# Attention and a gated feed-forward block on one core: batches 0 and 1 are transposed by TensorE and their reciprocals spread by a selector matmul

## The chip, the cores and the metric

The kernel runs on one core of a Trainium2 chip. The core has a matrix engine (TensorE, PE in the profile, with its weight loads as PEld), a vector engine (DVE), a scalar engine (ACT), a general engine (POOL) that here mainly issues loads, and a queue processor (SP) that issues the other transfers. The metric is the time of one execution on the device in microseconds.

## The reference

```python
B, H, S, D = q.shape                      # 8, 8, 576, 64
scores = scale * np.matmul(q, k.transpose(0, 1, 3, 2))
mask = (rel >= 0) & (rel < window)        # window 128
scores = np.where(mask, scores + bias[None], -1000000000.0)   # bias: -slope[h] * |rel|
attn = np.exp(scores - max)
attn = attn / (np.sum(attn, axis=-1, keepdims=True) + 1e-09)
x = (attn @ v), heads side by side        # 4608 tokens x 512
g = x @ w_gate                            # 512 x 1536
gelu = 0.5 * g * (1.0 + erf(g * inv_sqrt2))
val = x @ w_val                           # 512 x 1536
return (gelu * val @ w_out)               # 1536 x 512
```

Inputs and output are fp32.

## The kernel before

A batch (576 tokens) has five key blocks j of 128 keys; block 0 is half filled. Heads go in pairs, c = 0 to 3, with i the head in the pair. q, k and v of a batch are loaded by POOL with a cast to bf16 (L80, five loads each). Staging tiles `qs` and `ks` have one buffer; their transposes `qT`, `kT` have two. Batch 0 is transposed by TensorE (L101) and copied by DVE (L104), all others by a DMA transpose that SP issues (L110).

`scores0`, `scores1` and `scores2` compute the scores transposed, keys on partitions (L119). ACT takes the exp into `P` (L126), and DVE multiplies by the decay-and-window mask (L129), which comes in two layouts, `emask` and `emask2`. `sums` multiplies `P` by a block of ones, 48 matmuls of 32 columns each (L180), so that row 32c+16i and the 15 after it hold the sums of one head. DVE takes reciprocals (L187, L188) into `r`. To have each head's row on 64 partitions, SP writes eight rows of `r` to memory (`rd`, L192) and reads them back spread (`rb`, L194). `values` multiplies `P` by v (L205), and DVE scales the result with `rb` into `xT` (L211), the feed-forward's input, features on partitions.

The feed-forward goes in nine groups g of 512 tokens. `gate_val` makes one of twelve 128-feature steps f: four matmuls with `wg`, four with `wv` (L224), a gelu on ACT (L228), a product on DVE (L229). `out_half` is six matmuls with `wo` (L239); after two of them ACT copies the bank (L244) and SP stores it (L246). A group needs the attention of batches up to g (for g of 1 or more). Between the gates and the end of a group the program puts steps of the attention of later batches among the eight out halves.

The program sets the order on each engine; nothing reorders it. Every engine and SP's queue work through their instructions in turn. All matmul results go through eight PSUM banks handed out in turn by `bank()`, so a matmul can wait for the reader of a result eight banks earlier. POOL's loads have eight completion semaphores in turn, so a load waits for the one eight before. `P` has three buffers, each for two pairs.

The lines around which the start turns, before the loop over the groups (L303 to L315):

```python
load_qk(1)
load_v(0)
...
transposes_dma(1)
sums(0)
for n in range(4):
    todo.pop(0)[1]()
for c in range(4):
    values(0, c)
```

Of the kernel before, what the change touches and what calls it, by code (L numbers as in the profile page):

```python
# [19 lines left out]
PCOL = (512, 0, 256, 704, 960)  # L20

QS = 320
# [3 lines left out]
def kernel(  # L26
# [23 lines left out]
    p_pool = ctx.enter_context(tc.tile_pool(name="pp", bufs=3))  # L50
# [17 lines left out]
    ones = consts.tile([128, 2, 32], BF16, name="ones")  # L68
# [62 lines left out]
    def scores0(b, c):  # L131

        P = p_pool.tile([128, 2, 2, 1088], BF16, name="P")
        probs[b, c] = P
        ps = [bank(), bank()]
        for m in (0, 1):
            for i in (0, 1):
                score(b, c + m, i, 4, ps[i], 128 * m)
        for i in (0, 1):
            exp(P[:, :, i, 960:1088], ps[i][:, 0:256].rearrange("p (m n) -> p m n", m=2))  # L140

    def scores1(b, c):
        P = probs[b, c - c % 2][:, c % 2]
        ps = [bank(), bank()]
# [3 lines left out]
        for i in (0, 1):  # L148
            exp(P[:, i, 0:512], ps[i])
        mask(P[:, :, 0:512].rearrange("p i (n x) -> p i n x", n=2),  # L150
             emask[:, 2 * c:2 * c + 2, :].unsqueeze(2).to_broadcast((128, 2, 2, 256)))

    def scores2(b, c):
        P = probs[b, c - c % 2][:, c % 2]
        ps = [bank(), bank()]
        for j in (0, 3):
            for i in (0, 1):
                score(b, c, i, j, ps[i], 256 * (j // 3))
        for i in (0, 1):
# [13 lines left out]
    def sums(b):  # L173

        ps = [bank(), bank()]
        for j in range(5):
            for s, a, e, col in pieces(j):
                for i in (0, 1):
                    for c in range(4):
                        nc.tensor.matmul(  # L180
                            out=ps[s][32 * c:32 * c + 32, a - QS * s:e - QS * s],
                            lhsT=ones[:, i, :],
                            rhs=probs[b, c - c % 2][:, c % 2, i, col:col + e - a],
# [5 lines left out]
        rb = r_pool.tile([128, 4, S], FP32, name="rb")  # L189
        recip[b] = rb  # L190
        d = d_pool.tile([4, 2, S], FP32, name="rd")
        nc.sync.dma_start(out=d.rearrange("c i s -> (c i) s"), in_=r[0:128:16, :])  # L192
        for i in (0, 1):
            nc.sync.dma_start(  # L194
                out=rb[64 * i:64 * i + 64, :, :],
                in_=d[:, i, :].unsqueeze(0).to_broadcast((64, 4, S)))

    def values(b, c):
        P = probs[b, c - c % 2][:, c % 2]
        ps = [bank(), bank()]  # L200
# [49 lines left out]
    for t in (qs, ks):  # L250
# [3 lines left out]
        base=0, pattern=[[-1, 128]], channel_multiplier=1)  # L254
    load_qk(0)
    relt = consts.tile([128, 256], mybir.dt.int32, name="relt")
    tmpl = consts.tile([128, 256], FP32, name="tmpl")
    nc.gpsimd.iota(relt, pattern=[[1, 256]], base=0, channel_multiplier=-1)
    nc.gpsimd.tensor_copy(out=tmpl, in_=relt)
    for base, step, chan in ((0, 1, -1), (W - 1, -1, 1)):  # L260
        nc.gpsimd.affine_select(
            out=tmpl, in_=tmpl, compare_op=ALU.is_ge, fill=1e9,
            base=base, pattern=[[step, 256]], channel_multiplier=chan)
# [3 lines left out]
    nc.vector.memset(ones, 0.0)
    for i in range(2):
        nc.vector.memset(ones[:, i, 16 * i:16 * i + 16], 1.0)
    nc.vector.memset(emask2[0:64, :, 0:192], 0.0)  # L270

    def masks(c):
        for h in (2 * c, 2 * c + 1):
            slope = 2.0 ** (-8.0 * (h + 1) / H)
            nc.scalar.activation(out=emask[:, h, :], in_=tmpl, func=AF.Exp, scale=-slope)
        e, e2 = emask[:, 2 * c:2 * c + 2, :], emask2[:, 2 * c:2 * c + 2, :]
        nc.vector.tensor_copy(out=e2[64:128, :, 0:192], in_=e[64:128, :, 64:256])
        nc.vector.tensor_copy(out=e2[:, :, 192:448], in_=e)
# [105 lines left out]
```

## Time and profile before

| | us |
|---|---|
| median of 3 runs | 430.2 (428.4 to 431.09) |
| profiled execution, its own time | 431.19 |
| its span, first to last instruction | 429.4 |
| PE busy | 352.6 (82%) |
| DVE busy | 183.6 (43%) |
| ACT busy | 176.0 (41%) |
| POOL busy | 109.6 (26%) |
| mean granted clock of TensorE | 0.927 |

Busy shares are means over the whole span. They say little about a stretch in which all engines wait for one transfer; those are found in the page's slices and then in the timeline, in which each row gives a start, a duration, an instruction, and in brackets how long its engine stood before it and what ended that.

### The profile page before, as it was taken

Reading aid. Unit: us, or ns where it says so; the run is one execution under the profiler, and the core shown is the slowest. Engines: PE = TensorE matmul, PEld = TensorE weight load, DVE = VectorE, ACT = ScalarE, POOL = GpSimd, SP = SyncE. Lnnn points to the kernel's source line nnn. Section 1 sums busy time; section 2 is a strip of 40 time slices with the busy share of each in tenths; the row PEclk is TensorE's granted clock in tenths of the full one; section 3 lists DMA queues with packets and bytes.
Section 4 is the critical chain, followed back from the end, with each engine's and each line's share of the span. In section 5 each row is a group of like instructions: output and inputs, shape, how many; then the busy total and the mean of one; then the engine's idle time right before and its main releaser. Section 6 shows DMA issues by size and latency. Waiting matters only on the chain. (4 is left out here: it accounts for less than half of the span.)

```text
span 429.4 us, 6083 instructions
## 1 busy us (share of the span) xinstructions
PE 352.6 (82%) x2385; PEld 164.5 (38%) x2424; DVE 183.6 (43%) x281; ACT 176.0 (41%) x326; POOL 109.6 (26%) x138
## 2 busy tenths in 40 slices
PE   1640033997789697999999999999999999999996
PEld 0320031443334344444444344444444444444442
DVE  2580013245444466554645464545556450430330
ACT  1540031236533672428534842665285322322321
POOL 9394230917126103029005500920000000000000
PEclk9955556799989998999999999999999999999999
DMA  9499999999699939589679929994801502002002
GB/s 87 31 134 120 180 199 229 143 173 129 124 170 129 58 52 183 105 169 150 85 175 133 159 62 231 100 141 104 156 27 51 136 0 82 17 0 99 1 2 98
DMA packets 164269, 47.48 MB, mean 111 GB/s; under 512 B 149840, under 2 KB 155472, under 8 KB 164240
## 3 DMA queue, kind: packets, MB, share of 16 engines
q0 software_dynamic: 118288, 18.88, 59.3%
q1 hardware_dynamic: 45952, 28.20, 28.7%
q8 instruction: 19, 0.31, 0.3%
q14 instruction: 10, 0.08, 0.1%
HBM read 47.19 MB, written 9.58 MB: 132 GB/s over the span
## 5 line engine op out<-in xcount | busy, mean ns | idle before, releaser
L229 DVE TENSOR_TENSOR hT<-ps,gelu 128x512 bf16<-128x512 f32 x108 | 74.7, 691 | 126.4 <-PE ps L224 126.3
L224 PE MATMUL ps<-xT,wg 128*128 128x512 bf16 x431 | 114.1, 386 | 7.7 <-DMA wo<-in_moe_w_out_dram 6.9
L228 ACT ACTIVATE gelu<-ps 128x512 bf16<-128x512 f32 x108 | 64.5, 597 | 129.3 <-PE ps L224 129.0
L224 PE MATMUL ps<-xT,wv 128*128 128x512 bf16 x415 | 110.4, 384 | 0.7 <-issue 0.2
L239 PE MATMUL ps<-wo,hT 128*128 128x512 bf16 x411 | 99.8, 382 | 2.6 <-issue 1.9
L126 ACT ACTIVATE P<-ps 128x512 bf16<-128x512 f32 (+2 forms) x160 | 72.9, 555 | 46.8 <-PE ps L119 46.6
L129 DVE TENSOR_TENSOR P<-P,emask 128x1024 bf16<-128x1024 bf16 x64 | 46.0, 724 | 67.1 <-ACT P L126 67.1
L224 PEld LDWEIGHTS <-wg 128*128 128x128 bf16 x432 | 41.4, 99 | 58.9 <-issue 10.7
L224 PEld LDWEIGHTS <-wv 128*128 128x128 bf16 x432 | 42.8, 99 | 53.3 <-issue 3.1
L80 POOL DMA_DIRECT2D qs<-in_q_dram x40 | 33.7, 859 | 113.7 <-DMA qT<-qs 93.5
L239 PEld LDWEIGHTS <-hT 128*128 128x128 bf16 x432 | 38.7, 98 | 49.6 <-issue 9.4
L119 PE MATMUL ps<-qT,kT 64*128 64x256 bf16 (+1 forms) x320 | 27.4, 284 | 33.8 <-DMA qT<-qs 30.2
L244 ACT COPY osb<-ps 128x512 f32<-128x512 f32 x36 | 21.2, 588 | 63.2 <-PE ps L239 41.6
L80 POOL DMA_DIRECT2D vb<-in_v_dram x40 | 33.8, 894 | 47.5 <-PE ps L205 38.4
L211 DVE TENSOR_TENSOR xT<-ps,rb 128x320 bf16<-128x320 f32 x64 | 25.4, 449 | 21.7 <-DMA rb<-rd 20.9
L80 POOL DMA_DIRECT2D ks<-in_k_dram x40 | 33.8, 897 | 0.0
L119 PEld LDWEIGHTS <-kT 64*128 64x128 bf16 x320 | 11.7, 101 | 53.2 <-issue 47.8
L205 PE MATMUL ps<-P,vb 128*64 128x128 bf16 (+2 forms) x384 | 21.7, 259 | 3.7 <-DVE xT L211 3.7
L180 PE MATMUL ps<-P,ones 128*32 128x128 bf16 (+2 forms) x384 | 13.7, 270 | 13.4 <-DVE P L129 13.1
L205 PEld LDWEIGHTS <-vb 128*64 128x64 bf16 x384 | 16.0, 117 | 14.1 <-issue 13.8
L187 DVE RECIPROCAL r<-ps 128x320 f32<-128x320 f32 x8 | 17.3, 2157 | 5.7 <-PE ps L180 5.7
L180 PEld LDWEIGHTS <-ones 128*32 128x32 bf16 x384 | 10.2, 107 | 18.1 <-issue 17.9
(32 smaller groups left out, 65.7 us busy)
## 6 DMA issues: line engine op xcount, KB each, us to landing
rb<-rd SPq DMA_DIRECT2D x16, 576.0 KB, 7.9
out_dram<-osb SPq DMA_DIRECT2D x36, 256.0 KB, 5.0
qs<-in_q_dram POOLq DMA_DIRECT2D x32, 128.0 KB, 4.3
ks<-in_k_dram POOLq DMA_DIRECT2D x32, 128.0 KB, 4.4
vb<-in_v_dram POOLq DMA_DIRECT2D x32, 128.0 KB, 5.2
wg<-in_moe_w_gate_dram POOLq DMA_DIRECT2D x4, 384.0 KB, 21.0
wv<-in_moe_w_val_dram POOLq DMA_DIRECT2D x4, 384.0 KB, 23.0
wo<-in_moe_w_out_dram POOLq DMA_DIRECT2D x1, 1536.0 KB, 28.6
```

Source lines behind the costliest of these rows:

```text
L80: nc.gpsimd.dma_start(out=t[lo:128, j, :].rearrange("p (h d) -> p h d", h=H), in_=src[b][:, 128 * j - 64 + lo:128 * j + 64, :].rearrange(" ...
L119: nc.tensor.matmul(out=ps[:, col:col + 128 * n].rearrange("p (n t) -> p n t", n=n), lhsT=kT[b % 2][lo:lo + 64, j, c, :], rhs=qT[b % 2][lo: ...
L126: nc.scalar.activation(out=dst, in_=src, func=AF.Exp, scale=0.125)
L129: nc.vector.tensor_tensor(out=dst, in0=dst, in1=m, op=ALU.mult)
L180: nc.tensor.matmul(out=ps[s][32 * c:32 * c + 32, a - QS * s:e - QS * s], lhsT=ones[:, i, :], rhs=probs[b, c - c % 2][:, c % 2, i, col:col ...
L205: nc.tensor.matmul(out=ps[s][64 * i:64 * i + 64, a - QS * s:e - QS * s], lhsT=vb[b % 2][:, j, 64 * h:64 * h + 64], rhs=P[:, i, col:col + e ...
L211: nc.vector.tensor_tensor(out=xT[:, c, b * S + lo:b * S + hi], in0=ps[s][:, 0:hi - lo], in1=recip[b][:, c, lo:hi], op=ALU.mult)
L224: nc.tensor.matmul(out=ps, lhsT=w[:, c, 128 * f:128 * (f + 1)], rhs=xT[:, c, t0:t0 + 512], start=(c == 0), stop=(c == 3))
L228: nc.scalar.activation(out=gl, in_=pg, func=AF.Gelu)
L229: nc.vector.tensor_tensor(out=hid[g][:, f, :], in0=pv, in1=gl, op=ALU.mult)
L239: nc.tensor.matmul(out=po, lhsT=hid[g][:, f, 128 * t:128 * (t + 1)], rhs=wo[:, f, :], start=(f == 0), stop=(f == NF - 1))
L244: nc.scalar.copy(out=osb, in_=po)
```

## The change

Batches 0 and 1 are transposed by TensorE, and the copies of the transposes are shared between ACT and DVE. `qs` and `ks` get second buffers. Two ways now lead from `r` to `rb`: `spread_dma`, as before, for batches 2 to 7, and `spread_pe` for batches 0 and 1, eight fp32 matmuls with a constant 0/1 matrix `sel`, each copied out of its bank by ACT. The scores of a pair are made in one visit that takes four banks, and the scores of key block 4 of all four pairs in one visit of two. The mask has one layout: the block of ones for key block 0 holds zeros for the missing keys instead. `P` is per pair with six buffers. The order in the groups is written out as lists. From group 3 on, the sums of a batch stand after the first gate step and its values after the ninth and eleventh.

```diff
-    p_pool = ctx.enter_context(tc.tile_pool(name="pp", bufs=3))
+    p_pool = ctx.enter_context(tc.tile_pool(name="pp", bufs=6))
+    p4_pool = ctx.enter_context(tc.tile_pool(name="p4", bufs=2))
...
-    emask2 = consts.tile([128, H, 576], BF16, name="emask2")
+    sel = consts.tile([128, 4, 2, 64], FP32, name="sel")
-    qs, ks = (consts.tile([128, 5, DM], BF16, name=f"{nm}s") for nm in "qk")
+    qs, ks = ([consts.tile([128, 5, DM], BF16, name=f"{nm}s{i}") for i in range(2)]
+              for nm in "qk")
...
+    def scores0(b):
+        P = p4_pool.tile([128, 4, 2, 128], BF16, name="P4")
+        ps = [bank(), bank()]
+        for c in range(4):
+            for i in (0, 1):
+                score(b, c, i, 4, ps[i], 128 * c)
+        for i in (0, 1):
+            exp(P[:, :, i, :], ps[i].rearrange("p (c n) -> p c n", c=4))
+        mask(P.rearrange("p c i n -> p (c i) n"), emask[:, :, 0:128])
+    def scores(b, c):
+        ps = [bank() for _ in range(4)]
...
+        for n in (0, 1):
+            for i in (0, 1):
+                exp(P[:, i, 512 * n:512 * n + 512], ps[2 * n + i])
+            mask(P[:, :, 512 * n:512 * n + 512].rearrange("p i (n x) -> p i n x", n=2), e)
...
+    def spread_pe(b, r):
+        for lo, hi in ((0, QS), (QS, S)):
+            for c in range(4):
+                ps = bank()
+                nc.tensor.matmul(
+                    out=ps[:, 0:hi - lo], lhsT=sel[:, c, :, :].rearrange("p i m -> p (i m)"),
+                    rhs=r[:, lo:hi], start=True, stop=True)
+                nc.scalar.copy(out=recip[b][:, c, lo:hi], in_=ps[:, 0:hi - lo])
...
     load_qk(0)
+    load_qk(1)
+    load_v(0)
...
+    copies = (nc.scalar.copy, nc.vector.tensor_copy)
+    for c in (0, 1):
+        transposes(0, c, copies)
+    scores(0, 0)
+    for c in (2, 3):
+        transposes(0, c, (nc.vector.tensor_copy, nc.vector.tensor_copy))
+    scores0(0)
+    for c in (1, 2, 3):
+        scores(0, c)
...
-    transposes_dma(1)
-    sums(0)
-    for n in range(4):
-        todo.pop(0)[1]()
-    for c in range(4):
-        values(0, c)
+    r = sums(0)
+    for c in (0, 1):
+        transposes(1, c, (nc.scalar.copy, nc.scalar.copy))
+    spread_pe(0, r)
+    for c in range(4):
+        scale(0, c, values(0, c))
+    for c in (2, 3):
+        transposes(1, c, copies)
...
+            if 3 <= g < B - 1:
+                if f == 0:
+                    run(("sum", g + 1))
+                elif f in (8, 10):
+                    run(("pv", g + 1, f - 8, f - 7))
+        if g == 0:
+            todo = [("s0", 1), ("s", 1, 0), 0, 1, ("s", 1, 1), 2, 3, ("s", 1, 2), 4, ("s", 1, 3),
+                    5, 6, ("sum", 1), ("pv", 1, 0, 1, 2, 3), 7]
+        elif g == 1:
+            todo = [("s0", 2), ("s", 2, 0), 0, ("s", 2, 1), 1, ("s", 2, 2), 2, ("s", 2, 3), 3,
+                    ("s0", 3), 4, ("sum", 2), ("s", 3, 0), 5, 6, ("s", 3, 1), 7,
+                    ("pv", 2, 0, 1, 2, 3)]
+        elif g == 2:
+            todo = [("s", 3, 2), 0, ("s", 3, 3), 1, 2, ("s0", 4), ("sum", 3), ("s", 4, 0), 3, 4,
+                    ("s", 4, 1), 5, ("pv", 3, 0, 1), ("s", 4, 2), 6, ("pv", 3, 2, 3),
+                    ("s", 4, 3), 7]
+        elif b < B:
+            todo = [("s0", b), ("s", b, 0), 0, 1, ("s", b, 1), 2, 3, ("s", b, 2), 4, 5,
+                    ("s", b, 3), 6, 7]
```

Three places show what the lists move. The first is the start of SP's queue, before:

```order
L110 DMA_TRANSPOSE kT_93<-ks 128x20x128
L110 DMA_TRANSPOSE qT_91<-qs 128x20x128
L192 DMA rd<-r 8x576
L194 DMA rb<-rd 64x4x576 x2
L110 DMA_TRANSPOSE kT_92<-ks 128x20x128
L110 DMA_TRANSPOSE qT_90<-qs 128x20x128
L246 DMA out_dram<-osb 128x512
```

and now:

```order
L112 DMA_TRANSPOSE kT_97<-ks_93 128x20x128
L112 DMA_TRANSPOSE qT_95<-qs_91 128x20x128
L261 DMA out_dram<-osb 128x512 x4
L112 DMA_TRANSPOSE kT_98<-ks_94 128x20x128
L112 DMA_TRANSPOSE qT_96<-qs_92 128x20x128
L261 DMA out_dram<-osb 128x512 x2
L196 DMA rd<-r 8x576
```

Before, the queue began with the transposes of batch 1 and the reciprocals of batch 0. Now its first rows are the transposes of batch 2, and the first `rd` is that of batch 2.

The second is the same queue in the steady groups, one group before:

```order
L246 DMA out_dram<-osb 128x512
L110 DMA_TRANSPOSE kT_93<-ks 128x20x128
L110 DMA_TRANSPOSE qT_91<-qs 128x20x128
L246 DMA out_dram<-osb 128x512 x3
L192 DMA rd<-r 8x576
L194 DMA rb<-rd 64x4x576 x2
```

and now:

```order
L261 DMA out_dram<-osb 128x512 x3
L112 DMA_TRANSPOSE kT_98<-ks_94 128x20x128
L112 DMA_TRANSPOSE qT_96<-qs_92 128x20x128
L196 DMA rd<-r 8x576
L198 DMA rb<-rd 64x4x576 x2
L261 DMA out_dram<-osb 128x512 x4
```

`rd` and `rb` stood ahead of a group's last store and of the next group's transposes. They now stand behind both transposes.

The third is DVE after the gates of group 1, before (`emask_87` is the second mask layout):

```order
L129 TENSOR_TENSOR P<-P,emask 128x2x512
L129 TENSOR_TENSOR P<-P,emask_87 128x2x576
L187 RECIPROCAL r<-ps 128x320
L188 RECIPROCAL r<-ps 128x256
L129 TENSOR_TENSOR P<-P,emask 128x2x512
L129 TENSOR_TENSOR P<-P,emask_87 128x2x576
L129 TENSOR_TENSOR P<-P,emask 128x2x512
L129 TENSOR_TENSOR P<-P,emask_87 128x2x576
L211 TENSOR_TENSOR xT<-ps,rb 128x320
```

and now:

```order
L131 TENSOR_TENSOR P_1164<-P_1164,emask 128x1024
L131 TENSOR_TENSOR P<-P,emask 128x2x512 x8
L131 TENSOR_TENSOR P_1286<-P_1286,emask 128x1024
L189 RECIPROCAL r<-ps 128x320
L190 RECIPROCAL r<-ps 128x256
L131 TENSOR_TENSOR P<-P,emask 128x2x512 x4
L226 TENSOR_TENSOR xT<-ps,rb 128x320
```

Nine or ten masks now come before the reciprocals of batch 2, where four came before, and four masks still lie between the reciprocals and the first scaling.

## Rows read from the trace of the kernel before

**Rows 1.** Page, 40 equal slices: busy tenths of PE.
```profile
PE   1640033997789697999999999999999999999996
```

**Rows 2.** Timeline 0:75: start, duration, engine, line, instruction, count, [idle before <-releaser].
```profile
28.12 1.97 PE L180 MATMUL ps<-P,ones 128*32 128x192 bf16 x45 [2.13 <-DVE P L129]
...
35.98 14.72 SPq L110 DMA_TRANSPOSE qT<-qs  x1
...
60.33 2.10 PE L119 MATMUL ps<-qT,kT 64*128 64x128 bf16 x20 [30.24 <-DMA qT<-qs]
...
72.23 3.01 DVE L211 TENSOR_TENSOR xT<-ps,rb 128x320 bf16<-128x320 f32 x8 [6.33 <-DMA rb<-rd]
73.10 2.04 PE L224 MATMUL ps<-xT,wg 128*128 128x512 bf16 x3 [6.90 <-DMA wo<-in_moe_w_out_dram]
```

**Rows 3.** Timeline of POOL: template selects, loads and waits of the start.
```profile
10.81 0.86 POOL L261 TENSOR_SCALAR_AFFINE_SELECT tmpl<-tmpl 128x256 f32<-128x256 f32 x2
18.71 4.23 POOL L80 DMA_DIRECT2D qs<-in_q_dram  x5 [7.03 <-PE ps L101]
...
31.25 0.81 POOL L93 DMA_DIRECT2D wg<-in_moe_w_gate_dram  x1
...
49.15 0.69 POOL L80 DMA_DIRECT2D vb<-in_v_dram  x1 [1.27 <-DMA wv<-in_moe_w_val_dram]
...
64.09 0.88 POOL L80 DMA_DIRECT2D qs<-in_q_dram  x1 [1.22 <-DMA wv<-in_moe_w_val_dram]
```

**Rows 4.** Timeline 0:75: the first transposes and exps.
```profile
13.38 0.29 PE L101 MATMUL ps<-ident,ks 128*128 128x128 bf16 x1 [0.55 <-DMA ks<-in_k_dram]
...
13.46 0.74 PE L101 MATMUL ps<-ident,qs 128*128 128x128 bf16 x5
...
19.27 1.95 ACT L126 ACTIVATE P<-ps 128x512 bf16<-128x512 f32 x4
```

**Rows 5.** Lines by form: line, engine, operation, shapes, count | busy us, mean ns | idle.
```profile
L129 DVE TENSOR_TENSOR P<-P,emask 128x1024 bf16<-128x1024 bf16 x32 | 22.1, 691 | 51.7 <-ACT P L126 51.7
...
L244 ACT COPY osb<-ps 128x512 f32<-128x512 f32 x36 | 21.2, 588 | 63.2 <-PE ps L239 41.6 <-issue 21.7
...
L187 DVE RECIPROCAL r<-ps 128x320 f32<-128x320 f32 x8 | 17.3, 2157 | 5.7 <-PE ps L180 5.7
L188 DVE RECIPROCAL r<-ps 128x256 f32<-128x256 f32 x8 | 13.6, 1695 | 0.0
...
L126 ACT ACT_TABLE_LOAD x6 | 7.7, 1283 | 0.1
...
L104 DVE COPY qT<-ps 128x640 bf16<-128x640 bf16 x4 | 1.9, 486 | 6.9 <-PE ps L101 6.9
```

**Rows 6.** Windows: PE, PEld, DVE, ACT, POOL busy, PE clock, DMA share, GB/s.
```profile
120.00:125.00 5.00, 4.84 (x18) 1.98 (x17) 2.13 (x7) 2.47 (x3) 2.62 (x3) 0.66 1.18 82
```

**Rows 7.** Timelines 60:130 to 185:230: loop starts, and rd to scaled xT.
```profile
121.61 1.92 PE L224 MATMUL ps<-xT,wg 128*128 128x512 bf16 x4
...
154.65 0.62 SPq L192 DMA_DIRECT2D rd<-r  x1
...
164.84 1.55 DVE L211 TENSOR_TENSOR xT<-ps,rb 128x320 bf16<-128x320 f32 x4 [5.98 <-DMA rb<-rd]
...
172.82 1.03 PE L224 MATMUL ps<-xT,wg 128*128 128x512 bf16 x4
...
211.91 1.03 PE L224 MATMUL ps<-xT,wg 128*128 128x512 bf16 x4
```

**Rows 8.** Timeline 185:230: a transpose on SP's queue, a pair's values.
```profile
218.07 6.77 SPq L110 DMA_TRANSPOSE kT<-ks  x1
...
222.36 0.66 PE L205 MATMUL ps<-P,vb 128*64 128x192 bf16 x12
```

**Rows 9.** Timeline of PE from 340: the out matmuls of group 7, the first gates of group 8.
```profile
383.79 10.52 PE L239 MATMUL ps<-wo,hT 128*128 128x512 bf16 x47
394.15 1.03 PE L224 MATMUL ps<-xT,wg 128*128 128x512 bf16 x4
```

More of the change, by code (lines that the diff above doesn't have):

```diff
@@ L18 @@
 Q0 = (0, 64, 192, 320, 448)
[L20 removed]
+PCOL = (576, 0, 256, 768)
 QS = 320
@@ L95, in load_w, with transposes @@
                 in_=src[:, lo:hi].rearrange("(c p) f -> p c f", p=128))
-    def transposes(b, c):
-        for src, dst in ((qs, qT), (ks, kT)):
+    def transposes(b, c, copies):
+        for src, dst, copy in ((ks, kT, copies[0]), (qs, qT, copies[1])):
             ps = bank().bitcast(BF16)
@@ L176, in sums @@
         for j in range(5):
-            for s, a, e, col in pieces(j):
+            for s, a, e, lo in pieces(j):
                 for i in (0, 1):
@@ L254 @@
         base=0, pattern=[[-1, 128]], channel_multiplier=1)
-    load_qk(0)
[L256 to L263, printed above, removed]
+    tmpl = consts.tile([128, 256], FP32, name="tmpl")
@@ new lines @@
+    nc.gpsimd.iota(tmpl, pattern=[[1, 256]], base=0, channel_multiplier=-1,
+                   allow_small_or_imprecise_dtypes=True)
+    for half, base, step, chan in ((0, 0, 1, -1), (1, -1, -1, 1)):
+        t = tmpl[:, 128 * half:128 * half + 128]
+        nc.gpsimd.affine_select(
+            out=t, in_=t, compare_op=ALU.is_ge, fill=1e9,
+            base=base, pattern=[[step, 128]], channel_multiplier=chan)
+    load_qk(0)
+    load_qk(1)
+    load_v(0)
+    nc.vector.memset(ones, 0.0)
+    for i in range(2):
+        nc.vector.memset(ones[64:128, 0, i, 16 * i:16 * i + 16], 1.0)
+        nc.vector.memset(ones[:, 1, i, 16 * i:16 * i + 16], 1.0)
@@ L264 @@
+    nc.vector.memset(sel, 0.0)
     for i in range(2):
         nc.vector.memset(vb[i][0:64, 0, :], 0.0)
[L267 to L278, printed above, removed]
-        nc.vector.tensor_copy(out=e2[:, :, 448:576], in_=e[:, :, 0:128])
@@ L307, with run @@
         load_w(step * n, step * (n + 1))
-    nc.gpsimd.dma_start(out=wo, in_=moe_w_out.rearrange("(c p) f -> p c f", p=128))
-    load_v(1)
-    transposes_dma(1)
-    sums(0)
-    for n in range(4):
-        todo.pop(0)[1]()
-    for c in range(4):
-        values(0, c)
-    def fetch(b):
+    r = sums(0)
[6 more added lines that the diff above has]
+        transposes(1, c, copies)
+    for n in range(2):
+        nc.gpsimd.dma_start(
+            out=wo[:, 6 * n:6 * n + 6, :],
+            in_=moe_w_out[768 * n:768 * n + 768, :].rearrange("(c p) f -> p c f", p=128))
+    load_v(1)
+    def run(item):
+        what, b, *c = item
+        if what == "s0":
+            scores0(b)
+        elif what == "s":
+            scores(b, c[0])
+        elif what == "sum":
+            r = sums(b)
+            if b == 1:
+                spread_pe(b, r)
+            else:
+                spread_dma(b, r)
+        elif what == "pv":
+            for x in c:
+                scale(b, x, values(b, x))
+    for g in range(NG):
+        b = g + 2
         if b < B:
```

132 lines of the change are left out of this document (44 added, 88 removed).

## The prediction, made before the change was run

> **What bounds the kernel now.** I began with the slices of the page [rows 1]: TensorE (PE) is busy nine tenths or more from the seventeenth slice on, and nearly all of its idle time lies before that, in slices 1 to 7 and in a few dents up to 172 us. So the time is a start-up, three uneven groups of tokens, and a saturated rest. The timeline says what the start-up waits for [rows 2]: the sums of batch 0 end at 30.1, then PE stands for 30.2 us until the DMA transpose of qT lands. That transpose was issued at 35.98 and shares the DMA engines with the weights: these are issued from 31.25 on, and POOL's waits show wv's first quarter landed at 49.2 and its last at 64.1 [rows 3]. The reciprocals go through memory behind it, so xT comes at 72.2 and the first gate matmul starts at 73.1. From there I read the loop starts: gates of group 1 at 121.6, of group 2 at 172.8, of group 3 at 211.9 [rows 7]. The 39.1 us of the last interval repeats up to group 5. A pure group costs 48 out matmuls in 394.15 - 383.79 = 10.4 us [rows 9], 0.216 each, so 96 gate matmuls cost 20.7 and a group 31.1.
>
> **The new start, step by step.** Call T0 the first gate matmul (73.1 now).
> 1. iota and two selects now run ahead of the q loads. Two selects of twice the width took 0.86 [rows 3], so with the iota about 1.0 us. The last k tile was transposed at 13.4 [rows 4]; now 14.4. Fifteen transposes follow; five took 0.74 with their tail [rows 4], so about 2.0: done at 16.4.
> 2. First exps at 16.9. Four exps take 1.95 [rows 4]: 18.9, mask 0.69 [rows 5]: 19.6. Then DVE copies four transposes at 0.49 [rows 5]: 21.5. Only then can the scores of key block 4 run (all four pairs), so ACT stands about 3 us, and works 14 exps at 0.49 = 6.9 from 22.0 to 28.9; last mask 29.6. The twelve copies that built the second mask are gone from DVE, but ACT is the slower here, and they gain nothing.
> 3. Sums: 1.97 at low clock [rows 2], the first reciprocal starts 1.2 into them: 30.8 + 2.16 + 1.70 [rows 5] = 34.7. Meanwhile PE makes 20 transposes of batch 1, about 3 us, to 34.6: they hide the reciprocals.
> 4. The spread: eight fp32 matmuls, each copied out by ACT. No row shows an fp32 matmul. Lower end: one pass like bf16, 0.216 x 320/512 and x 256/512, 1.0 us for eight. Upper end: a column as dear as in the slowest fp32 row, the reciprocals, 4 x (2.16 + 1.70) = 15.4. I take 4.0, half a microsecond each, near the copy of 512 fp32 columns at 0.59 [rows 5], because each product must leave by such a copy: 38.6. The Trainium skill (FP8 and Floating Point Precision, TensorE Precision Notes) says that true FP32 takes four passes through the array. By it the eight cost an estimated 3.9 us at the full clock and 7.8 at half; the sum would then be the same or 3.8 higher.
> 5. Values of four pairs, 0.66 each at full clock [rows 8], somewhat more here: 3.1, to 41.7. DVE scales a pair in 0.78 (four pieces in 1.55 [rows 7]), hidden but for the last. Twenty transposes of batch 1 stand ahead of the gates: 2.3. **T0 = 44.0**, 29.1 earlier.
>
> Do the loads keep up? POOL stood 7.0 us before q of batch 1, for the one buffer of q and k [rows 3]; with a second one it doesn't, so the weights are issued from 24.5, not 31.25. Six quarters took 64.1 - 49.2 = 14.9, 2.5 each, so from about 31 to 49; a pair of quarters feeds three gate steps, 5.2 us. No wait if that pace holds.
>
> **The groups after it** (t from the last gate matmul; sums at full clock 1.1; scores of a batch 9,216 columns, two heads side by side, 2.1).
> - Group 0: PE work is scores 2.1, out 10.4, sums 1.1, spread 4.0, values 2.6 = 20.2. ACT needs 1.3 for its table [rows 5], 0.5 for the last gelu, 8.8 for 18 exps and about 1 for two copies, so the last mask comes 1.1 after PE wants it; then PE stands 1.8 for the first reciprocal, as nothing lies between sums and spread. 23.1 + 20.7 = 43.8, against 48.5 now, which held a slow start (its first three gate matmuls took 2.04 [rows 2]) and two waits.
> - Group 1: sums of batch 2 start at 12.2 (ACT again); the reciprocals wait for a mask, end at 17.4. From rd's issue to the first scaled xT took 164.84 - 154.65 = 10.2 [rows 7]: 27.6. PE has then long made the rest and all four values (20.8): it stands 7.6. Scaling follows pair by pair, the first gate ends about 1.6 late, and after such a stop the clock is low: behind the stop that ended group 0 it was 0.66 from 120 to 125 [rows 6], worth 1.7. 31.5 + 20.7 = 52.2, against 51.2.
> - Group 2: sums of batch 3 start at 6.5 and rb is used at 22.2. PE gets to the third score of batch 4 by 14.3, where the banks held by two unscaled values stop it for 8.3. Then 4.4 of work, 27.0, and 1.5 for the clock. 49.2, **against 39.1**: the change gives back 10 here, because a batch and a half of scores stand in it and the way of the reciprocals through memory is no longer covered by gates.
> - Groups 3 to 5: 31.1 + sums 1.1 + values 2.6 + scores 2.1 + 0.6 = 37.5, against 39.1; the difference is the wait of the sums for the last mask. Here rd stands on SP behind both transposes: the first took 6.8 on the queue [rows 8] with rb in flight ahead, the second less, so rd goes at 8 to 10.5 into the loop, and scaled xT comes at 18 to 20.7. PE would stop for it only from about 20.5, when the third pair's values want banks. I take no stop.
> - Groups 6, 7, 8: 34.8 + 31.1 + 31.1 = 97.0, last copy and store 4.0 (429.4 less the end of the last out matmul, 394.2 + 31.1), against 34.0 (what is left of the span) + 62.2 + 4.0.
>
> Differences: start -29.1, group 0 -4.7, group 1 +1.0, group 2 +10.1, groups 3 to 5 -4.8, group 6 +0.8: **-26.7**. Against the profiled execution, 431.2 us with a span of 429.4, that is 404.5; the median of the runs is 1.0 lower, so **404 us**.
>
> **Rivals.**
> - A. The fp32 products stream several times while the clock is low. For: the 48 sums took 1.97 there [rows 2], near twice what the columns cost at 0.216 per 512. Against: sums and transposes keep PE busy for 5 us before. Doubling the 4.0 taken above: T0 +4, 408. Chance 0.15. The rule on four passes quoted from the Trainium skill in step 4 would make it so.
> - B. The loads set the start after all: then the wait for the transpose only hid one for the weights. For: in this trace wv's first quarter landed at 49.2 [rows 3]. Against: it was issued 7 us later than it will be, beside two DMA transposes that are gone. T0 = 49.2 and some microseconds for wo, which would come last: 409 to 414. Chance 0.12.
> - C. rb comes later than 20.5 into groups 3 to 6 by 1 to 3 us: four times that, 408 to 416. Chance 0.10.
> - D. **Slower than before**: the same place on SP, but rd and rb fall behind transposes as slow as qT's first, which took 24 us from issue to use [rows 2]. The point is the 20.5 us above; each microsecond beyond it costs four in sum, and +31 is reached when scaled xT comes 28 into the loop. 435. Against: that one shared the engines with all the weights, a later one took 6.8 on the queue [rows 8]. Chance 0.02.
> - E. Better than summed: PE slips past the stop in group 2, or starts at 40: 393 to 399. Chance 0.13.
> Left for the forecast, 399 to 408: 0.45; 0.03 for the upper end of the fp32 cost, +11 at each spread (427).
>
> A change under 1% cannot be told from none here. Faster by over 1%: all but D and a part of the last and of what I overlook, 0.94; same 0.03; slower 0.03. The range 393 to 416 takes in E, A, B and most of C.
>
> **What will show it.** The 30 us hole of PE after the sums gone, and gates from about 44 (48 says A, 49 with waits on wg or wv says B). Eight fp32 matmuls near 0.5 us each. DVE waiting on rb before xT at the end of groups 1 and 2, with PE idle about 8 us in each, and a low clock behind it. Loops of 37.5 in groups 3 to 5, with DVE but not PE waiting for rb (PE waiting says C). The forecast fails if the stops of groups 1 and 2 are missing, or if T0 lies outside 40 to 49.

## The result, and the profile after the change

| | before | after |
|---|---|---|
| median, us | 430.1 (4 runs, 428.4 to 431.1) | 408.7 (4 runs, 406.6 to 409.6) |
| profiled execution, its own time | 431.19 | 409.64 |
| its span | 429.4 | 407.8 |
| PE busy | 352.6 (82%) | 359.6 (88%) |
| mean granted clock of TensorE | 0.927 | 0.944 |

The ratio of after to before is 0.9499, 95% interval 0.9452 to 0.9547: 21.4 us faster. The forecast was 404, its range 393 to 416. The time lies inside the range, and the sum still holds one large error.

The table gives the start of the first gate matmul and then the length of each group's loop, gate start to gate start, in us. All rows but the predicted one are read from timelines of PE.

| | first gate | g0 | g1 | g2 | g3 | g4 | g5 | g6 | g7 |
|---|---|---|---|---|---|---|---|---|---|
| before | 73.1 | 48.5 | 51.2 | 39.1 | 39.1 | 39.1 | 39.1 | 33.9 | 31.1 |
| predicted | 44.0 | 43.8 | 52.2 | 49.2 | 37.5 | 37.5 | 37.5 | 34.8 | 31.1 |
| after | 41.0 | 43.2 | 49.0 | 51.4 | **47.6** | 37.4 | 37.4 | 34.6 | 31.1 |

So the start gave 32.1 us and groups 2 and 3 gave 12.3 and 8.5 of that back. Groups 0, 1, 4 and 5 are shorter by 5.3, 2.2, 1.7 and 1.7, and group 6 is longer by 0.7. Group 3 should have been one of three equal loops and is 10.2 longer than its neighbours.

First the slices of the page of after, which answer to [rows 1]. Each digit is the busy share of a fortieth of the span in tenths; PEclk is the granted clock.

```profile
PE   0569999899992899949929999999999999999996
...
PEclk9958999999997699979977999999999999999999
...
DMA  9999999999918990199959984967110502002002
```

The hole of slices 4 to 7 is gone. Three dents are left, in slices 13, 18 and 21 (about 130, 180 and 210 us), each with a low clock beside it. The last one is new: nothing stood there before.

The start, from the timeline of all engines (start, duration, engine, line, instruction, count, idle before and its releaser); it answers to [rows 2]:

```profile
29.14 1.97 PE L183 MATMUL ps<-P,ones 128*32 128x192 bf16 x45 [1.64 <-DVE P L131]
...
30.30 2.16 DVE L189 RECIPROCAL r<-ps 128x320 f32<-128x320 f32 x1 [1.21 <-PE ps L183]
...
33.16 4.77 PE L206 MATMUL ps<-r,sel 128*128 128x320 f32 x16
...
37.86 2.06 PE L217 MATMUL ps<-P,vb 128*64 128x192 bf16 x48
...
40.98 1.03 PE L239 MATMUL ps<-xT,wg 128*128 128x512 bf16 x4
```

PE doesn't stop between the sums and the gates. The spread takes 4.77 us; the profile counts two instructions for each product, so x16 are the eight of the code. It starts at 33.16, behind the first twenty transposes of batch 1, which hide the reciprocals: those of the first 320 columns are there at 32.46, and the first four products need no others.

POOL's timeline at the same time, which answers to [rows 3]:

```profile
23.79 0.95 POOL L96 DMA_DIRECT2D wg<-in_moe_w_gate_dram  x1
...
30.23 0.83 POOL L319 DMA_DIRECT2D wo<-in_moe_w_out_dram  x1 [0.30 <-DMA wg<-in_moe_w_gate_dram]
32.17 0.82 POOL L319 DMA_DIRECT2D wo<-in_moe_w_out_dram  x1 [1.11 <-DMA wv<-in_moe_w_val_dram]
```

The weights are issued 7.5 us earlier. Their first quarters have landed by 30.2 and 32.2, where wv's landed at 49.2 before. The gates don't wait for them.

PE's timelines around the dents:

```profile
133.21 2.77 PE L239 MATMUL ps<-xT,wg 128*128 128x512 bf16 x4 [8.59 <-DVE xT L226]
...
140.62 1.03 PE L239 MATMUL ps<-xT,wg 128*128 128x512 bf16 x4
...
179.69 0.64 PE L217 MATMUL ps<-P,vb 128*64 128x128 bf16 x6 [5.12 <-DVE xT L226]
...
213.78 2.02 PE L217 MATMUL ps<-P,vb 128*64 128x192 bf16 x24 [7.65 <-DVE xT L226]
215.74 1.89 PE L239 MATMUL ps<-xT,wg 128*128 128x512 bf16 x4
```

The first stop ends group 1 (8.59), the second lies in group 2 (5.12), the third in group 3 (7.65). All three wait for a scaled xT. The 16 gate matmuls behind the first one took 140.62 - 133.21 = 7.4 us, where 16 at 0.216 are 3.5. Around the third stop the clock was low too, by the windows (PE, PEld, DVE, ACT, POOL busy, then the granted clock):

```profile
212.00:217.00 5.00, 3.22 (x28) 2.12 (x28) 3.77 (x9) 0.00 (x0) 1.65 (x3) 0.50 0.07 6
```

DVE's timeline says what the scaling before the third stop waited for:

```profile
213.23 1.55 DVE L226 TENSOR_TENSOR xT<-ps,rb 128x320 bf16<-128x320 f32 x4 [10.92 <-DMA rb<-rd]
```

So what is late stands on SP's queue. Its timeline in group 3 (from 184.6) and in group 4 (from 232.2), which answers to [rows 8]:

```profile
186.06 5.87 SPq L112 DMA_TRANSPOSE kT<-ks  x1
192.09 7.40 SPq L112 DMA_TRANSPOSE qT<-qs  x1
199.55 1.24 SPq L196 DMA_DIRECT2D rd<-r  x1
205.45 1.25 SPq L198 DMA_DIRECT2D rb<-rd  x2
...
233.58 3.21 SPq L112 DMA_TRANSPOSE kT<-ks  x1
236.92 3.51 SPq L112 DMA_TRANSPOSE qT<-qs  x1
240.96 0.63 SPq L196 DMA_DIRECT2D rd<-r  x1
243.12 1.26 SPq L198 DMA_DIRECT2D rb<-rd  x2
```

The same chain runs at about half the speed in group 3. The two transposes take 13.3 us instead of 6.7, and from rd to rb it is 5.9 instead of 2.2. POOL's timeline shows what else is under way: the loads of q and k for batch 6 go out during the transposes of batch 5, while those for the next batch are all issued 5.7 us before the transposes of group 4.

```profile
182.90 4.21 POOL L83 DMA_DIRECT2D qs<-in_q_dram  x5
187.04 4.26 POOL L83 DMA_DIRECT2D ks<-in_k_dram  x5
...
219.50 4.23 POOL L83 DMA_DIRECT2D qs<-in_q_dram  x5
223.64 4.26 POOL L83 DMA_DIRECT2D ks<-in_k_dram  x5
```

The view of the DMA queues for 186 to 199 us (packets, MB, share of the span of 16 engines) says that both are served at once, POOL's on the first queue and SP's on the second. The shares add up to 180.7%, so packets overlap on the 16 engines:

```profile
q0 software_dynamic: 7569, 0.95, 119.6%
q1 hardware_dynamic: 3361, 1.08, 61.1%
```

The Trainium skill (DMA: Bandwidth & Descriptors, Issuing engines are not separate DMA queues) says that transfers issued by different engines end on the same 16 DMA engines and interleave there. The two rows agree with it; the price for the transposes is that of the timelines.

### The profile page after: what moved, and what is told of

Same layout as the page of the kernel before. It is cut to its first block, busy times and chain, and to the rows that moved or that the text cites. A ratio compares the mean times of both kernels' runs of the same rounds, so it can differ in the third digit from the quotient of the medians.

```text
span 407.8 us, 6271 instructions
## 1 busy us (share of the span) xinstructions
PE 359.6 (88%) x2496; PEld 175.2 (43%) x2496; DVE 181.9 (45%) x281; ACT 188.8 (46%) x334; POOL 110.2 (27%) x139
## 4 chain that ended last, share of the span: by engine, by line
PE 75%; DMA 9%; ACT 7%; DVE 4%; POOL 2%; issue 1%; SPq 0%; DVEq 0%; POOLq 0%; ACTq 0%
PE ps L239 45%; PE ps L254 19%; ACT P L128 6%; DMA rb<-rd 6%; PE ps L217 3%; PE ps L121 3%; DMA rd<-r 2%; PE ps L206 2%; PE ps L183 2%; DVE r L189 2%; PE ps L104 1%; POOL qs L83 1%; DMA ks<-in_k_dram 1%; DVE xT L226 1%; POOL ks L83 1%
## 5 line engine op out<-in xcount | busy, mean ns | idle before, releaser
L239 PE MATMUL ps<-xT,wv 128*128 128x512 bf16 x432 | 113.0, 385 | 0.0
L128 ACT ACTIVATE P<-ps 128x512 bf16<-128x512 f32 x144 | 74.3, 640 | 13.6 <-PE ps L121 13.6
L131 DVE TENSOR_TENSOR P<-P,emask 128x1024 bf16<-128x1024 bf16 x72 | 49.3, 695 | 36.0 <-ACT P L128 36.0
L254 PEld LDWEIGHTS <-hT 128*128 128x128 bf16 x432 | 40.2, 98 | 51.4 <-issue 7.4
L226 DVE TENSOR_TENSOR xT<-ps,rb 128x320 bf16<-128x320 f32 x64 | 24.5, 449 | 37.0 <-DMA rb<-rd 28.2
L217 PE MATMUL ps<-P,vb 128*64 128x128 bf16 (+2 forms) x384 | 18.8, 252 | 12.8 <-DVE xT L226 12.8
L121 PE MATMUL ps<-qT,kT 64*128 64x256 bf16 (+1 forms) x320 | 25.7, 277 | 3.0 <-DVE qT L107 2.2
L121 PEld LDWEIGHTS <-kT 64*128 64x128 bf16 x320 | 13.0, 98 | 18.6 <-issue 15.3
L189 DVE RECIPROCAL r<-ps 128x320 f32<-128x320 f32 x8 | 17.2, 2151 | 2.0 <-PE ps L183 2.0
L104 PE MATMUL ps<-ident,ks 128*128 128x128 bf16 x40 | 5.6, 272 | 13.1 <-DMA ks<-in_k_dram 13.1
L183 PE MATMUL ps<-P,ones 128*32 128x128 bf16 (+2 forms) x384 | 11.3, 256 | 3.9 <-DVE P L131 3.9
```

Source lines behind the costliest of these rows:

```text
L121: nc.tensor.matmul(out=ps[:, col:col + 128 * n].rearrange("p (n t) -> p n t", n=n), lhsT=kT[b % 2][lo:lo + 64, j, c, :], rhs=qT[b % 2][lo: ...
L128: nc.scalar.activation(out=dst, in_=src, func=AF.Exp, scale=0.125)
L131: nc.vector.tensor_tensor(out=dst, in0=dst, in1=m, op=ALU.mult)
L189: nc.vector.reciprocal(r[:, 0:QS], ps[0][:, 0:QS])
L217: nc.tensor.matmul(out=ps[s][64 * i:64 * i + 64, a - QS * s:e - QS * s], lhsT=vb[b % 2][:, j, 64 * h:64 * h + 64], rhs=prob(b, c, i, j, lo ...
L226: nc.vector.tensor_tensor(out=xT[:, c, b * S + lo:b * S + hi], in0=ps[s][:, 0:hi - lo], in1=recip[b][:, c, lo:hi], op=ALU.mult)
```

## The experiments

Every kernel here computes the whole reference. Ratios are to the kernel before, on the same chip, with their 95% intervals. The experiments ran on three chips, on which the median of before was 429.3 to 429.7 us (430.1 in the result above), so medians of different chips are set side by side in the text.

**The loads of batch 6 kept away from the transposes.** The value load of group 3, and with it the q and k loads behind it on POOL, is held back until the last hidden tile of the group is written:

```diff
...
-            load_v(b)
+            if g != 3:
+                load_v(b)
...
+        if g == 3:
+            nc.gpsimd.tensor_copy(out=late, in_=hid[g][:, NF - 1, 0:2])
+            load_v(b)
```

> Group 3 alone is changed: POOL starts the loads of v of batch 5 and of q and k of batch 6 only when the last hidden tile of the group is there. Theory 1 (the 10 us lost in group 3, 47.6 against 37.4 in groups 4 and 5, come from these loads sharing the DMA engines with the two transposes, rd and rb): rd within 9 to 11 us of the group's first gate, xT within 21, no stop of PE, group 3 at 37.5 to 38.5, the whole 9 to 10 us shorter, 399. Theory 2 (the place of rd behind both transposes on SP is enough): rd still at 15, group 3 at 47, 408.7. Theory 3 (the late values of group 2 carry over): no change either.

Measured: 416.1 us, ratio 0.9679 (0.9636 to 0.9722), slower than after. The loops are 40.6 | 43.2 48.5 51.8 **37.4 55.2** 37.4 34.6 31.1. SP's timeline in groups 3 and 4:

```profile
185.52 3.13 SPq L112 DMA_TRANSPOSE kT<-ks  x1
188.81 3.10 SPq L112 DMA_TRANSPOSE qT<-qs  x1
191.96 0.61 SPq L196 DMA_DIRECT2D rd<-r  x1
193.96 1.25 SPq L198 DMA_DIRECT2D rb<-rd  x2
...
229.44 6.69 SPq L112 DMA_TRANSPOSE kT<-ks  x1
236.26 7.64 SPq L112 DMA_TRANSPOSE qT<-qs  x1
```

Group 3 is healed, by 10.2 us: without the loads the transposes take 3.1 each and there is no stop. But the loads held back, and those of the next batch behind them, now go out from 209.8 to 237.6 and meet the transposes of group 4, which loses 17.8. The total went the other way than expected, since the expectation had not asked where the loads would land; the mechanism shows in both groups.

**The first spread by memory.** Only batch 0 goes back to rd and rb:

```diff
-    spread_pe(0, r)
+    spread_dma(0, r)
```

> Batch 0 goes through memory again, all else as changed. Theory 1 (the spread by TensorE is a real part of the earlier start): rd leaves at 34, rb shares the engines with the weights and takes 10 to 20 us, so xT at 46 to 55 instead of 38.4, the first gate at 47 to 56 instead of 41.0, the whole 6 to 15 us longer: 415 to 424. Rival (only the order, batch 1 taken out from ahead of the gates, made the start earlier, and rb is quick once no transposes stand before it): first gate at 43 to 45, 411 to 413.

Measured: 421.1 us, ratio 0.9781 (0.9727 to 0.9835), 12.4 over after. The first gate comes at 53.7 instead of 41.0. PE's timeline:

```profile
51.60 0.69 PE L104 MATMUL ps<-ident,ks 128*128 128x128 bf16 x5 [16.65 <-DVE xT L226]
```

Beside the weights the way through memory (rd at 33.96, rb at 39.08, xT at 51.06) costs PE a stop of 16.65; the fp32 products cost 4.8.

**Batch 1 by DMA transpose.** Only the forty TensorE transposes of batch 1 go back:

```diff
-    for c in (0, 1):
-        transposes(1, c, (nc.scalar.copy, nc.scalar.copy))
+    transposes_dma(1)
...
-    for c in (2, 3):
-        transposes(1, c, copies)
```

> Batch 1 is transposed by DMA again, at the place where its transposes by TensorE began; its scores stay behind the gates of group 0. Theory 1 (what made PE stand 30 us was the order, scores of batch 1 ahead of the values of batch 0; the transposes themselves have until 62): first gate at 40 to 43, the whole within 2 us of the changed kernel: 407 to 411. Rival (the DMA transposes hold up the weights as before, where the first quarter of wv landed 17 us after its issue): wg and wv first at 42 or later, then waits at every third gate step, first gate 43 to 49 and the whole 413 to 420.

Measured: 412.4 us, ratio 0.9601 (0.9552 to 0.9650), 3.7 over after. The first gate is no later (40.5): the first spread now waits 1.5 and takes 6.21 instead of 4.77 (granted clock 0.66), since no transposes cover the reciprocal, but the transposes behind it are gone too. The loss is in the loops: 45.9 and 50.1 instead of 43.2 and 49.0; in the first of them the second spread, behind the same wait of 1.81 as in after, takes 5.84 at a granted clock of 0.71 instead of 4.15 at 1.00. The rest of the loss was not traced. SP's timeline at the start:

```profile
22.75 5.26 SPq L112 DMA_TRANSPOSE kT<-ks  x1
28.13 11.79 SPq L112 DMA_TRANSPOSE qT<-qs  x1
```

Here the other transfers are the weights, and qT takes 11.8. That run's wg lands at 33.9 instead of 30.2.

**Neither part.** Both go back, the TensorE transposes of batch 1 and the spread of batch 0. The new order of the work, the mask, the buffers, the four-bank visits and the spread of batch 1 by TensorE stay:

```diff
+    transposes_dma(1)
     r = sums(0)
-    for c in (0, 1):
-        transposes(1, c, (nc.scalar.copy, nc.scalar.copy))
-    spread_pe(0, r)
+    spread_dma(0, r)
```

(and the two lines of the other transposes, as above).

> Batch 1 is transposed by DMA and batch 0 spread through memory, with rd behind the two transposes on SP as in the kernel before; batch 1's scores stay behind the gates of group 0. If the two parts only add (+12.4 and +3.7 by themselves): 425. If the one makes the other worse (rd and rb behind transposes that share the engines with the weights): first gate at 60 to 72, the whole 427 to 440, so that without both parts the new order alone gains nothing.

Measured: 432.2 us in 10 runs, ratio 1.0085 (1.0054 to 1.0117): 0.9% slower than before. The loops are 61.5 | 47.9 48.4 50.3 46.9 37.4 37.4 34.6 31.1. SP's timeline, and behind it PE's:

```profile
39.69 0.71 SPq L196 DMA_DIRECT2D rd<-r  x1
49.14 1.31 SPq L198 DMA_DIRECT2D rb<-rd  x2
```

```profile
61.55 2.77 PE L239 MATMUL ps<-xT,wg 128*128 128x512 bf16 x4 [27.25 <-DVE xT L226]
```

rd stands behind qT until 39.7, rb goes 9.4 later, and PE stands 27.3. The two parts need each other: one alone undone costs 12.4 or 3.7, both cost 23.5. What stays brings the first gate 11.6 earlier and loses more than that in groups 2 and 3 (11.2 and 7.8). Which of its pieces brings the 11.6 was not tried apart, and the spread of batch 1 was not undone by itself.

**The sums before the gates again.** From group 3 on, the sums stand before the last out half, as they did before the change, so that rd goes ahead of the transposes:

```diff
-                if f == 0:
-                    run(("sum", g + 1))
-                elif f in (8, 10):
+                if f in (8, 10):
...
-                    ("s", b, 3), 6, 7]
+                    ("s", b, 3), 6, ("sum", b), 7]
```

(and one entry for batch 4 in the list of group 2).

> From batch 4 on the sums stand one step from the end of the group before, not behind the first gate step; rd and rb so stand ahead of the transposes on SP. Theory 1 (what groups 3 to 5 gained over the kernel before, 39.1 to 37.4, is the wait of the sums for the last mask, now covered by a gate step): groups 4 and 5 go back to 38.5 to 39.1, and group 3, whose rb then leaves ahead of the loads, falls from 47.6 to about 39; the whole 5 to 7 us shorter, 402 to 404. Rival (the gain came from the one visit of four banks): groups 4 and 5 stay at 37.4.

Measured: 406.1 us, ratio 0.9434 (0.9387 to 0.9481); its interval and that of after overlap, and the 402 to 404 expected were missed. Loops 39.7 | 43.2 49.3 55.2 39.6 38.9 38.9 33.4 31.1. In group 3 rd now goes at 187.92 and rb at 191.47, ahead of the transposes (10.4 us for the two there), and PE doesn't wait for a scaled xT in that group: the slow transposes cost something only to what stands behind them. But group 2 is 3.8 longer, since the sums of batch 4 now stand in it, behind a wait of 2.20 for the last mask. The steady groups cost 1.5 more, and PE's timeline has the reason, in groups 4 and 5 as in this row from the end of group 3:

```profile
224.69 1.10 PE L183 MATMUL ps<-P,ones 128*32 128x192 bf16 x45 [1.23 <-DVE P L131]
```

The sums wait 1.23 for the last mask. That bears out most of the 1.6 us which the prediction gave to groups 3 to 5 for moving the sums behind a gate step.

**Batches 2 and 3 spread by TensorE too.**

```diff
-            if b == 1:
+            if b <= 3:
```

> Batches 2 and 3 are spread by TensorE too, directly behind their sums. Theory 1 (the stops of 8.6 us in group 1 and 5.1 in group 2 are the way of the reciprocals through memory): both stops and the low clock behind them go; PE pays 2.4 for the first reciprocal and 4.1 for eight products in each. Group 1 49.0 to about 44.5, group 2 51.4 to about 50, group 3 as it is: about 403. Rival (the stop only moves to the scaling on DVE, or to waiting for the copies on ACT): 407 to 410.

Measured: 408.9 us, ratio 0.9509 (0.9470 to 0.9547), the same as after, which the expectation missed. Groups 1, 2 and 3 are 48.5, 50.5 and 49.1 (after 49.0, 51.4 and 47.6). PE's timeline and the windows of the two spreads:

```profile
119.60 5.67 PE L206 MATMUL ps<-r,sel 128*128 128x320 f32 x16 [2.44 <-DVE r L189]
...
164.34 7.18 PE L206 MATMUL ps<-r,sel 128*128 128x320 f32 x16 [2.49 <-DVE r L189]
```

```profile
119.60:125.20 5.60, 5.60 (x16) 3.89 (x18) 1.55 (x1) 2.77 (x7) 0.00 (x0) 0.72 0.00 0
164.30:171.40 7.10, 7.06 (x16) 4.80 (x16) 1.59 (x1) 2.73 (x7) 0.00 (x0) 0.56 0.00 0
```

The stops for rb are gone. But the product follows the sums directly, so PE stands 2.4 for the reciprocal, and the clock granted to the products is 0.72 and 0.56. A wait of 2.4 with slow products behind it costs about what the memory's wait cost.

**The spread of batches 2 and 3, a few steps later.** The products become an entry of their own in the lists, a pair's scores and two out halves behind their sums:

```diff
...
-                    ("s0", 3), 4, ("sum", 2), ("s", 3, 0), 5, 6, ("s", 3, 1), 7,
+                    ("s0", 3), 4, ("sum", 2), ("s", 3, 0), 5, 6, ("sp", 2), ("s", 3, 1), 7,
...
-            todo = [("s", 3, 2), 0, ("s", 3, 3), 1, 2, ("s0", 4), ("sum", 3), ("s", 4, 0), 3, 4,
+            todo = [("s", 3, 2), 0, ("s", 3, 3), 1, 2, ("s0", 4), ("sum", 3), ("s", 4, 0), 3, 4, ("sp", 3),
```

> Batches 2 and 3 spread by TensorE, but three steps behind their sums (score and two out halves between), so that the first product waits for no reciprocal and the clock stays up. Theory 1 (in the version with the spread directly behind the sums it cost 2.4 of waiting and 5.7 to 7.2 at a low clock, as much as the stop it took away): spread 4.1 each, no wait; group 1 49.0 to 45, group 2 51.4 to 45, group 3 still 47 to 49: 398 to 400. Rival (ACT's copies or the scaling on DVE then set the end of the groups): 405 or more.

Measured: 397.8 us, ratio 0.9248 (0.9193 to 0.9303). PE's timeline:

```profile
119.51 4.04 PE L206 MATMUL ps<-r,sel 128*128 128x320 f32 x16
...
159.96 4.04 PE L206 MATMUL ps<-r,sel 128*128 128x320 f32 x16
```

No wait, 4.04 each, at a granted clock of 1.00 in both windows. Groups 1 and 2 fall to 44.3 and 44.7. Against the kernel that had the same products directly behind the sums, group 1 gains 4.2: 2.4 of wait and 1.6 of slower products.

**The loads early, with a third buffer for v.** So that v's load needn't wait for the values, and only the load of group 4 is held:

```diff
-    vb = [consts.tile([128, 5, DM], BF16, name=f"vb{i}") for i in range(2)]
+    vb = [consts.tile([128, 5, DM], BF16, name=f"vb{i}") for i in range(3)]
...
+            if g == 4:
+                nc.gpsimd.tensor_copy(out=late, in_=hid[3][:, NF - 1, 0:2])
```

> v gets a third buffer, so that v of batch 5 and q and k of batch 6 are loaded during group 2; v of batch 6 and q and k of batch 7 wait for the last hidden tile of group 3. No load then runs beside the transposes, rd and rb of groups 3 to 5. Theory (the loads' share of the DMA engines is what costs, in whatever group they meet the transposes): groups 3, 4 and 5 at 37.4 each, the whole 10 us shorter, 398 to 400. Rival (the third buffer only moves the meeting to group 2, whose rb comes later): group 2 longer by several us, the whole 403 or more.

Measured: 410.1 us, ratio 0.9525 (0.9468 to 0.9582): no gain, so the expectation missed. Group 3 is 38.3, group 2 is no longer than in after (50.1), and group 4 is 46.4: the meeting has moved by one group, with the same stop of PE (7.65 for a scaled xT). POOL's held loads go out from 209.6 on, and SP's timeline has the transposes of group 4 beside them:

```profile
222.66 6.83 SPq L112 DMA_TRANSPOSE kT<-ks  x1
229.62 8.19 SPq L112 DMA_TRANSPOSE qT<-qs  x1
```

**Both of these.**

> The later spread of batches 2 and 3 and the early loads together. If the two losses are separate they add: 408.7 - 10 - 10 = 389, groups 3 to 5 at 37.4. If one hides the other: 396 to 399.

Measured: 397.3 us, ratio 0.9230 (0.9185 to 0.9276): what the later spread gives alone. Loops 41.0 | 43.2 44.3 44.8 37.4 **46.4** 37.4 34.6 31.1. In group 4 POOL issues q and k loads until 211.5 and v loads of the next batch from there to 216.2, and SP's queue reaches the transposes in between:

```profile
212.03 7.99 SPq L112 DMA_TRANSPOSE kT<-ks  x1
220.12 7.00 SPq L112 DMA_TRANSPOSE qT<-qs  x1
```

They take 15.0 us, rd goes at 227.2, and PE stands 7.3 for a scaled xT. The loads were early enough for group 3 and not for group 4.

**The loads clear of the transposes in both groups.** Against the last kernel, the hold stands two gate steps earlier, and for group 5 too:

```diff
-            if g == 4:
-                nc.gpsimd.tensor_copy(out=late, in_=hid[3][:, NF - 1, 0:2])
+            if g in (4, 5):
+                nc.gpsimd.tensor_copy(out=late, in_=hid[g - 1][:, 9, 0:2])
```

> Later spread of batches 2 and 3, three buffers for v, and two holds on POOL: v of batch 6 with q and k of batch 7 wait for the tenth hidden tile of group 3, v of batch 7 for that of group 4. The loads then end before the next group's transposes begin. Theory (a meeting of loads with transposes and rd costs 9 to 10 us wherever it falls, and nothing else is left there): groups 3, 4 and 5 at 37.4 each, the whole 388 to 390. Rival (it only moves on, into group 5, or the landing of the last loads still meets the transposes of group 4): one of the groups at 40 to 47, 391 to 398.

Measured: **387.9 us**, ratio 0.9031 (0.8973 to 0.9090), faster than both kernels. Loops 41.3 | 43.2 44.3 44.7 37.4 37.4 37.4 34.6 31.1. SP's timeline in group 4:

```profile
212.31 3.51 SPq L112 DMA_TRANSPOSE kT<-ks  x1
215.93 3.69 SPq L112 DMA_TRANSPOSE qT<-qs  x1
219.71 0.61 SPq L196 DMA_DIRECT2D rd<-r  x1
221.62 1.26 SPq L198 DMA_DIRECT2D rb<-rd  x2
```

POOL's q and k loads went out from 199.3 to 207.8, 3.7 us earlier than in the kernel just before, and the next v loads only at 232.5. kT falls from 7.99 to 3.51, the stop is gone, group 4 gains 9.0 us, and the total 9.4. Which of the two, the earlier q and k or the later v, did more was not tried apart.

**A pair's scores in two visits.** From group 3 on, two banks at a time with an out half between:

```diff
...
-            todo = [("s0", b), ("s", b, 0), 0, 1, ("s", b, 1), 2, 3, ("s", b, 2), 4, 5,
-                    ("s", b, 3), 6, 7]
+            todo = [("s0", b), ("h", b, 0, 0), ("h", b, 0, 1), 0, ("h", b, 1, 0), 1,
+                    ("h", b, 1, 1), 2, ("h", b, 2, 0), 3, ("h", b, 2, 1), 4, ("h", b, 3, 0), 5,
+                    ("h", b, 3, 1), 6, 7]
```

> From group 3 on the scores of a pair go in two visits of two banks with an out half between them, as in the kernel before; at the other places the matmuls come in the changed kernel's order. Theory 1 (the one visit of four banks is worth nothing by itself): groups 4 and 5 at 37.3 to 37.6, the whole within 1 us of the changed kernel, 408 to 410. Rival (four banks at once let ACT run without gaps and so bring the last mask earlier): groups 4 and 5 at 38 to 39, 411 or more.

Measured: 409.5 us, ratio 0.9538 (0.9482 to 0.9595), not to be told from after. Groups 4 and 5 are 38.0 instead of 37.4, so the single visit of four banks is worth about 0.6 a group, and the stop in group 3 is there as before (6.46).

**One buffer for q and k of batches 0 and 1**, so that batch 1 is loaded only after batch 0 has been transposed:

```diff
...
+    def qk(b):
+        return max(b - 1, 0) % 2
...
-    load_qk(1)
-    load_v(0)
```

(the two loads stand behind the scores of batch 0 instead).

> At the start q and k of batch 1 use the buffer of batch 0 again, so that their loads, and behind them v and the weights, wait on POOL for the transposes of batch 0; later batches take the two buffers in turn. Theory 1 (the weights had room: a pair of quarters lands every 4 us and is used up in 5.2): weights issued 7 us later, first gate still at 41, the whole 408 to 410. Rival (the second buffer is what lets the first gates come at 41): first gate at 45 to 48, or waits on wg, wv or wo in group 0, 413 to 417.

Measured: 409.8 us, ratio 0.9559 (0.9498 to 0.9619), not to be told from after. POOL stands 7.5 us and issues the weights from 31.5 instead of 23.8, and the first gate still comes at 40.8. So the weights had at least 7.7 us to spare, and the second buffer gave the start nothing.

## Why the prediction was right, and where it was not

**The start: right, 3.0 too late.** 41.0 against 44.0. The reciprocals were hidden behind the transposes as said, and the spread started 1.5 earlier than summed: it needs the first half of the reciprocals alone, and the transposes before it took 2.1 instead of 3. The spread itself, taken as 4.0, was 4.8; the values took 2.1 instead of 3.1 and the last twenty transposes 1.1 instead of 2.3.

**The fp32 products: the value taken was right, its reason was not.** Eight took 4.04 at a granted clock of 1.00, 3.0 above the lower end and 11.4 below the upper. The reason given for 4.0 was the copy by which each product leaves. But time times granted clock is nearly the same in all rows (4.04 x 1.00, 5.67 x 0.72, 7.18 x 0.56, all 4.0 to 4.1), so TensorE's own clock sets the pace and not ACT's copies; as far as that reason goes, the hit was luck. The Trainium skill (FP8 and Floating Point Precision, TensorE Precision Notes) has true FP32 in four passes. By it eight products of 320 and 256 columns are an estimated 3.8 at 2.4 GHz; the row of 4.04 agrees. Rival A expected them at the lower clock at the start, 8 us. That did not happen there (4.77). What a stop before them can cost shows elsewhere: 7.18 behind one of 2.49, though behind one of 1.81 they took 4.15 in after and 5.84 with batch 1 transposed by DMA.

**The loads: right, rival B falls.** The weights could go out 7.7 us later and still not delay the gates. Its point against itself, that the slow landing of [rows 3] belonged to a queue with two transposes beside it, is in part what undoing that part showed: wv's first quarter lands 7.6 after its issue in after, 12.9 with the two DMA transposes back, 17.2 in before.

**Groups 0 to 2: right within 2 us in sum.** They were summed as 43.8, 52.2 and 49.2 and came as 43.2, 49.0 and 51.4. Group 1 is shorter and group 2 longer mostly because the late scaling and the low clock lie behind the first gate matmul, so in the next loop, where I had put them into the loop that ends with it. The stops are 8.6 and 5.1, against 7.6 and 8.3. The one in group 2 is shorter mostly because PE comes to it later, 16.6 behind the last gate matmul instead of 14.3; it ends at 21.7 instead of 22.6. That the change gives some 10 back in group 2, because the way through memory has no gates over it, agrees with the later spread of batches 2 and 3, which takes 4.7 and 6.7 out of groups 1 and 2 although it adds 4.04 of products to each.

**Groups 3 to 5: the failing step, "I take no stop".** For groups 4 and 5 it holds (37.4 against 37.5; the first scaling starts 19.0 into group 4). For group 3 it cost 10.1 us: 47.6. The limit of 20.5 us was right, since PE stood from 21.5 on. What was wrong is "the second less": the two transposes took 13.3 together, rd went at 15.0 into the loop instead of 8 to 10.5, and the scaling came at 28.6. I had taken 6.8 for the first from [rows 8], a row with an rb in flight ahead and no loads beside it, and had not asked which loads POOL would issue here. This is rival C's place, with another size and count: one group by 8 us and a low clock behind it, not four groups by 1 to 3. That the loads beside the transposes are the cause is shown three times, by the kernel that moved them out of group 3 (37.4, with the loss turning up in group 4), by the one that moved the meeting to group 4, and by the one that cleared both. In the last, group 3 to 5 are what the sum had for all three.

**The rest: right.** Groups 6 and 7 came as 34.6 and 31.1.

**Rival D** came about in one group of its four: scaled xT came 28.6 into group 3, where D had 28, behind transposes of 13.3 together. In groups 4 and 5 it came at 19.0 and 18.7, so the whole stayed far from D's 435. The kernel with neither part came near D's picture at the start, with rd behind a qT beside all the weights, and lands 0.9% above before. **Rival E**, 393 to 399, needed the stop of group 2 to vanish or a start at 40; the stop came, and what the start of 41.0 won went in group 3. So the errors were -3.0 at the start, -1.6 in groups 0 to 2, +10.1 in group 3 and about -0.4 behind it; they leave +5.1 in the profiled execution, 409.6 against 404.5.

What stays open is where the transposes lose their time beside the loads. Packets of both queues run on the same engines at once, but whether it is these engines or the memory behind them was not tried.

## What to carry to other kernels

When a step moves behind a transfer on a queue, price that transfer with the traffic that will run beside it, group by group: the buffer that comes free decides which loads go out, and one steady group can differ from the next. Moving loads out of the way of a latency chain pays only if the place where they land is free as well; follow them one group further before counting the gain. A tiny round trip through memory can be replaced by a selector matmul for 4 us, but only with other work between it and the result it needs.

## What the runs showed of the hardware that was not expected

- A DMA transpose of a batch took 3.0 to 4.1 us in groups 3 to 5 where no loads ran beside it and no rb ahead of it (2.7 to 3.4 as the second of two in before), 5.4 to 8.8 there beside the loads of a batch, and up to 11.8 beside the weights in the changed kernels (14.7 in before, [rows 2]). From rd's issue to rb's it was 1.8 to 2.3 without loads, 3.3 to 6.0 beside them, and 5.1 to 9.7 beside the weights.
- fp32 products of 128x320 and 128x256 take 4.04 for eight at a granted clock of 1.00, and 7.18 at 0.56 behind a stop of only 2.5 us. The time goes with the granted clock, and the wait alone doesn't say what clock follows: behind 1.81 it was 1.00 in one kernel and 0.71 in another. Behind the stop of 8.6 the next 16 bf16 matmuls took 7.4 instead of 3.5.
- The kernel without the two parts was no faster than the kernel before (ratio 1.0085), though the two parts together are worth 23.5 on top of it.
